# Gates of two steps as one pair in an attention and rational feed-forward kernel, with a planned order of work

## The chip, the cores and the metric

The kernel runs on one core of a Trainium2 chip. TensorE (PE in the profile; PEld are its weight loads), VectorE (DVE), ScalarE (ACT), GpSimd (POOL) and SyncE (SP, which issues the transfers here) run their own queues in order and wait for each other through semaphores. The metric is the device time of one execution in microseconds, median of several runs.

## What is computed

Sliding-window attention (8 batches, 8 heads, 576 positions, head size 64, window 64) gives x with 4608 tokens of 512 columns. A feed-forward layer with a rational gate follows:

```python
def _moe_ref(x, w_in, w_out, a, b) -> np.ndarray:
    h = x @ w_in
    h2 = h * h
    h3 = h2 * h
    P = a[0] + a[1] * h + a[2] * h2 + a[3] * h3
    Q = 1.0 + np.abs(b[0]) * np.abs(h) + np.abs(b[1]) * h2
    g = P / (Q + 1e-06)
    return (g @ w_out).astype(np.float32)
```

The hidden width is 2048, the output has 512 columns, all in float32.

## The kernel before

**Tiles and steps.** The tokens are cut into 12 chunks of 384 (CH). A chunk needs 4 attention units (one for each pair of heads) and 16 steps (one for each 128 of the hidden width). All products of the feed-forward layer are made in three terms of split operands (high and low parts of x, w and g), which keeps float32 accuracy. A step has ffn1 (l. 517: 12 matmuls of 128x384 into a PSUM bank h), the gate (l. 529 to 543) and ffn2 (l. 550: 9 matmuls of 128x512 into three banks ps_o). Chunks 0 and 1 go first over one half of the hidden width and then the other (l. 545), so that the second half of the weights can be loaded and split meanwhile; the sums of a half are spilled to memory and read back. From chunk 2 on all weights stay in SBUF.

**The gate.** ScalarE reads h three times: u = h squared, r = |b0 h|, num = a3 h + a2. DVE makes u = |b1| u + r. ScalarE takes 1/(1 + 1e-6 + u) as Ln and Exp into r. DVE makes num = num h, then num = (num + a1) h, the last read of h; then gh = (num + a0) r, and in three more operations the low part gl. That is five ScalarE and seven DVE operations of 128x384 a step. u, r and num have two tiles each, gh and gl four each (GB), h two banks.

**Attention units.** A unit loads qk and v (l. 389, 397; two slots each), makes scores in the two banks ps_s, takes the row maximum on DVE, Exp on ScalarE into sm, normalizes sm on DVE (l. 467), transposes it on TensorE into ps_s, copies that to pT on ScalarE (l. 475; one tile), multiplies with v into ps_x and splits the result into xh and xl (l. 488 to 502). From chunk 3 on, a unit's value products and the next one's scores are one group (l. 508).

**Weights.** load_weight (l. 370) takes a loaded slot w_st (three, after six spare places at the start): ScalarE extracts exponents into top, DVE puts the words together in a tile w_c (two of them), ScalarE rounds that to the high part, DVE subtracts for the low part. Then fetch() issues the next load. There are 32 such pieces, two in each of the first steps, then one.

**The order of work.** Nothing is issued as it is written. Each call is recorded with what it reads and writes (Planner, l. 51), a cost is put on it (l. 110), and plan() (l. 183) simulates the engines: whenever an engine is free it takes, of the operations that are ready, the one recorded first. emit() then issues each engine's queue in that order. ffn1 and the gate of a step are recorded at step s, ffn2 of step s at s + 3 (LAG). A dependence is recorded between a write and a read or two writes of the same bytes; two reads make none.

Of the kernel before, what the change touches and what calls it, by code (L numbers as in the profile page):

```python
# [21 lines left out]
CH = 384  # L22
# [1 line left out]
PR = TC // 2  # L24
AHEAD = 3
LAG = 3
GB = 4
SLOTS = 3
WARM = 7
FILL = 430  # L30
C1AT = 0, 0, 1, 3
ON_PE = 2
JOIN = 4
# [17 lines left out]
class Planner:  # L51
# [58 lines left out]
    def cost(self, engine, method, out, reads, kw, args):  # L110
        if isinstance(out, Late):
            n = out.size // 4
        else:
            n = 1
            for _, k in out.ap[1:]:
                n *= k
        if engine == "SP":
            parts = 128 if isinstance(out, Late) else (out.ap[0][1] if out.tensor.__class__.__name__ != "DRamTensorHandle" else 0)
            size = mybir.dt.size(out.dtype) * n * (parts or out.ap[0][1])
            return 400, 400, size  # L120
        if engine == "PE":
            if method == "transpose":
                return 109, 270, 0
            if isinstance(args[2], Late):
                n = args[2].size // 4
            else:
                n = 1
                for _, k in args[2].ap[1:]:
                    n *= k
                if args[2].dtype == F32:  # L130
                    return (45, 270, 0) if args[1].ap[0][1] == 64 else (52, 225, 0)
            return n * 0.452, n * 0.452 + 165, 0
        if engine == "ACT":
# [23 lines left out]
        if engine == "POOL":  # L157
            return (n * 2.0 + 60, n * 2.0 + 100, 0) if method in ("tensor_scalar", "tensor_copy") else (n * 2.4 + 130, n * 2.4 + 170, 0)
# [24 lines left out]
    def plan(self):  # L183
        waiting = {e: [] for e in self.free}
        missing = [len(o.before) for o in self.ops]
        for o in self.ops:
            if not o.before:
                waiting[o.engine].append(o)
        dma_free = 0
        for _ in self.ops:  # L190
            start, engine = min((max(self.free[e], min(o.ready for o in w)), e) for e, w in waiting.items() if w)
            op = min((o for o in waiting[engine] if o.ready <= start), key=lambda o: o.index)
            waiting[engine].remove(op)
            op.start, self.free[engine] = start, start + op.occ
# [53 lines left out]
def swa_rational_ffn(ctx: ExitStack, tc: tile.TileContext, qk, v, w_in, w_out, out):  # L248
# [16 lines left out]
    ps_s = psum.tile([P, 2, 512], F32, name="ps_s")  # L265
    ps_x = psum.tile([P, 512], F32, name="ps_x")
    ps_o = [psum.tile([P, DO], F32, name=f"o{t}") for t in range(NTS)]
    h_ring = Ring(psum, 2, [P, 512], F32, "h")


    ctx.enter_context(tc.manual_schedule())
# [31 lines left out]
    a_sb, b_raw = ab_sb[:, 0:4], ab_sb[:, 4:6]  # L303
    b_sb = const.tile([P, 2], F32, name="b_sb")

    warm = const.tile([P, 512], BF16, name="warm")
    nc.vector.memset(warm, 0.0)
    for _ in range(WARM):
        nc.tensor.matmul(ps_o[2], warm[:, 0:P], warm, start=True, stop=True)
    make_mask()  # L310

    H = NF // 2
# [24 lines left out]
    QK = 2 * CH + WIN  # L337
    QKAB = QK + 6
    UNIT = QKAB + TC * P
    qk_ring = Ring(ring, 2, [P, QKAB], F32, "qk")  # L340
    vt_ring = Ring(ring, 2, [P, TC * P], F32, "vt")
    w_ring = Ring(ring, SLOTS, [P, 1026], F32, "w_st")
    spare = [late.tile([P, H * NCC * P], F32, name=f"early_{n}", tag=f"late_{n}") for n in ("wi_h", "wi_l")]
    spare_slots = [t[:, k * 1026:(k + 1) * 1026] for k in range(H * NCC * P // 1026) for t in spare]
    c_ring = Ring(ring, 2, [P, 512], F32, "w_c")
    top_ring = Ring(const, 0, [], F32, "top")
    top_ring.tiles = tops
    sm_ring = Ring(ring, 2, [P, 2, PR, P], F32, "sm")
    pT_ring = Ring(ring, 1, [P, 2, PR * P], F32, "pT")
    small = {n: Ring(ring, 2, [P, 2 * PR], F32, n) for n in ("nmx", "sums", "rs")}  # L350
    tmp = {n: Ring(ring, 2, [P, CH], F32, n) for n in ("r", "u", "num")}
    g_ring = [Ring(ring, GB, [P, CH], F32R, n) for n in ("gh", "gl")]
    ob_ring = Ring(ring, 2, [P, DO], F32, "ob")

    shares = {t.tensor.name: f"late_{n}" for t, n in zip(early + spare, ("wo_l", "wo_h", "wi_h", "wi_l"))}
# [14 lines left out]
    def load_weight(which, i):  # L370
        w = staged.pop((which, i))
        f = (lambda t: t.rearrange("p c n -> p (c n)")) if which == "in" else (lambda t: t)
        hi_name, lo_name = ("wi_h", "wi_l") if which == "in" else ("wo_h", "wo_l")
        top, c = top_ring(), c_ring()
        low = w.bitcast(U32)[:, 0:1024].rearrange("p (n two) -> p n two", two=2)[:, :, 1]
        exponents = w.bitcast(BF16)[:, 4:2052].rearrange("p (n four) -> p n four", four=4)[:, :, 0]
        pl.scalar.copy(out=top.bitcast(F16).rearrange("p (n two) -> p n two", two=2)[:, :, 1], in_=exponents)
# [9 lines left out]
        return c if c < 2 else (c + 1) % 2  # L387

    def load_qk(c, hp):
        qk_t = early[hp // 2][:, hp % 2 * UNIT:hp % 2 * UNIT + QKAB] if c == 0 else qk_ring()  # L390
        pl.sync.dma_start(out=qk_t, in_=qk[hp, c])
        u = live[c, hp] = {}
        u["q"] = qk_t[:, 0:CH].rearrange("p (t s) -> p t s", s=WIN)
# [12 lines left out]
    def two_banks(c, hp, transposed):  # L406
        if c == 0 and transposed:
            return [ps_o[0], ps_o[1]], None
        if c == 0 and hp % 2:
            return [h_ring(), h_ring()], None  # L410
        return [ps_s[:, 0], ps_s[:, 1]], ps_s

    def blocks(ap):
# [26 lines left out]
    def score_maximum(c, hp):  # L440
        u = live[c, hp]
        on_pe, ps, both, m = u["on_pe"], u["ps"], u["both"], u["m"]
        sm, nmx = u["sm"], u["nmx"] = sm_ring(), small["nmx"]().rearrange("p (z r) -> p z r", z=2)
        if not on_pe:
            u["s"] = [sm[:, z] for z in range(2)]
            for z in range(2):
# [20 lines left out]
    def unit_norm(c, hp):  # L467
# [2 lines left out]
        pl.vector.tensor_scalar(out=u["sums"], in0=u["sums"], scalar1=1e-9, scalar2=None, op0=ALU.add)  # L470
        pl.vector.reciprocal(out=rs, in_=u["sums"])
        sm = u["sm"] = u["sm"].rearrange("p z r c -> p (z r) c")
        pl.vector.tensor_tensor(out=sm, in0=sm, in1=rs.unsqueeze(2).broadcast_to([P, 2 * PR, P]), op=ALU.mult)

    def unit_transpose(c, hp):
        u = live[c, hp]
        ps, both = two_banks(c, hp, True)
        with pl.group():
            for j in range(2 * PR):
                pl.tensor.transpose(ps[j // PR][:, (j % PR) * P:(j % PR + 1) * P], u["sm"][:, j, :], ident)  # L480
        pT = u["pT"] = pT_ring()
        if both is not None:
            pl.scalar.copy(out=pT, in_=both[:, :, 0:PR * P])
        else:
# [29 lines left out]

    gs = {}

    def ffn1(c, i):
        h = h_ring()[:, 0:CH]
        n = 0
        whole = ExitStack()  # L520
        if c > 1 or i >= 2:
# [1 line left out]
        with whole:  # L523
            for cc in range(NCC):
                with pl.group():
                    for w, x in (("wi_h", 1), ("wi_h", 0), ("wi_l", 0)):
                        pl.tensor.matmul(h, weight_piece(w, i, cc), x_sb[x_slot(c)][x][cc], start=n == 0, stop=n == 3 * NCC - 1)
                        n += 1
        r, u, num = (tmp[n]() for n in ("r", "u", "num"))
        gh, gl = (g() for g in g_ring)  # L530
        pl.scalar.activation(u, h, AF.Square)
        pl.scalar.activation(r, h, AF.Abs, scale=b_raw[:, 0:1])
        pl.scalar.activation(num, h, AF.Identity, scale=a_sb[:, 3:4], bias=a_sb[:, 2:3])
        pl.vector.scalar_tensor_tensor(out=u, in0=u, scalar=b_sb[:, 1:2], in1=r, op0=ALU.mult, op1=ALU.add)
        pl.scalar.activation(r, u, AF.Ln, bias=QADD)
        pl.scalar.activation(r, r, AF.Exp, scale=-1.0)
        pl.vector.tensor_tensor(out=num, in0=num, in1=h, op=ALU.mult)
        pl.vector.scalar_tensor_tensor(out=num, in0=num, scalar=a_sb[:, 1:2], in1=h, op0=ALU.add, op1=ALU.mult)
        pl.vector.scalar_tensor_tensor(out=gh, in0=num, scalar=a_sb[:, 0:1], in1=r, op0=ALU.add, op1=ALU.mult)
        pl.vector.scalar_tensor_tensor(out=u, in0=u, scalar=QADD, in1=gh.bitcast(F32), op0=ALU.add, op1=ALU.mult)  # L540
        pl.vector.scalar_tensor_tensor(out=u, in0=num, scalar=a_sb[:, 0:1], in1=u, op0=ALU.add, op1=ALU.subtract)
        pl.vector.tensor_tensor(out=gl, in0=u, in1=r, op=ALU.mult)
        gs[c, i] = gh, gl

    phases = [(0, 0, H), (1, 0, H), (1, H, NF), (0, H, NF)] + [(c, 0, NF) for c in range(2, NCH)]
# [94 lines left out]
    for s in range(total + LAG):  # L640
# [1 line left out]
            if fn is load_weight:  # L642
                fn(*args)
        if s < total:
            ffn1(*steps[s])
        for fn, *args in todo.get(s, ()):
            if fn is not load_weight:
                fn(*args)
        if s >= LAG:
            ffn2(s - LAG)  # L650
    pl.plan()
    pl.fill("PE", ps_o[2].tensor.name, FILL, (nc.tensor.matmul, (ps_o[2], warm[:, 0:P], warm), dict(start=True, stop=True)))
    pl.emit()


# [35 lines left out]
```

## Time and profile before

| | |
|---|---|
| median of 3 runs | 982.49 us (981.6 to 982.84) |
| the profiled execution | 982.07 us |
| its span, first to last instruction | 980.3 us |
| TensorE matmuls | 952.6 us busy, 97% |
| DVE | 911.2 us busy, 93% |
| ScalarE | 698.5 us busy, 71% |
| granted TensorE clock | 0.997 of full speed |
| DMA | 68.38 MB, mean 70 GB/s |

Matmuls are pipelined and their ends are modelled, so their busy time says only whether TensorE had something to do. A duration is that of one instruction; neighbours on an engine overlap by some tens of ns, so the distance from start to start is what an instruction takes of its engine. All recorded operations carry line 226 in the profile (the planner's emit), so they are told apart by their tiles: `num<-num,h` is DVE's first product of the gate. In the list of waits a row says which engine and tile waited for which, the total in us, how often, and the longest.

### The profile page before, as it was taken

The page shows a single profiled execution, that of the slowest core. Times are in us where ns is not written, and L with a number is a line of the kernel's source. Part 1 is how long each engine was busy: PE and PEld are TensorE (multiplying, and loading weights), DVE is VectorE, ACT ScalarE, POOL GpSimd, SP SyncE. Part 2 cuts the span into 40 slices and gives each one's busy share as a digit, 9 for nine tenths or more (in the row PEclk, how much of TensorE's full clock was granted, in tenths as well). Part 3 has the DMA queues.
Part 4 walks back from the last instruction along what each step waited for, and adds up shares of the span by engine and source line. Part 5 has one row for each costly group of instructions (what it writes and reads, how often), then busy time and mean ns, then how long its engine had stood idle before and what let it go on. Part 6 is the DMA issues. An engine that isn't in the chain of part 4 may idle for free.

```text
span 980.3 us, 17701 instructions
## 1 busy us (share of the span) xinstructions
PE 952.6 (97%) x6672; PEld 824.6 (84%) x6675; DVE 911.2 (93%) x1747; ACT 698.5 (71%) x1737; POOL 4.4 (0%) x20
## 2 busy tenths in 40 slices
PE   8899999999999999999999999999999999999998
PEld 5677788888888888888888888888888888888996
DVE  6999999998999999999999999999999899999996
ACT  7988777776667667767677677667766776676664
POOL 1000000000000000000000000000000000000000
PEclk9999999999999999999999999999999999999999
DMA  9344341313103103103102200210310310300000
GB/s 360 127 171 147 122 150 39 96 50 117 51 1 117 35 17 118 35 17 116 37 17 74 79 17 26 93 51 1 118 35 17 118 35 18 100 1 2 33 1 32
DMA packets 24564, 68.38 MB, mean 70 GB/s; under 512 B 2720, under 2 KB 2720, under 8 KB 24480
## 3 DMA queue, kind: packets, MB, share of 16 engines
q1 hardware_dynamic: 24480, 67.27, 20.2%
q8 instruction: 52, 0.85, 0.4%
q14 instruction: 32, 0.26, 0.1%
HBM read 57.03 MB, written 10.22 MB: 69 GB/s over the span
## 4 chain that ended last, share of the span: by engine, by line
PE 64%; DVE 19%; ACT 10%; issue 2%; DMA 1%; ACTq 0%; DVEq 0%
PE o L226 29%; PE h L226 28%; DVE u L226 6%; PE ps_s L226 5%; ACT sm L226 4%; DVE num L226 3%; PE ps_x L226 3%; ACT r L226 2%; DVE gh L226 2%; DVE sm L226 2%; DVE nmx L226 1%; ACT u L226 1%; DVE gl L226 1%; DMA w_st<-w_out 1%; ACT num L226 1%
## 5 line engine op out<-in xcount | busy, mean ns | idle before, releaser
L226 PE MATMUL h<-xl,wi_h 128*128 128x384 f32 x768 | 260.4, 339 | 7.7 <-DVE num L226 6.2
L226 PE MATMUL h<-xh,wi_l 128*128 128x384 f32 x768 | 258.1, 336 | 0.0
L226 PE MATMUL h<-xh,wi_h 128*128 128x384 f32 x768 | 257.9, 336 | 0.0
L226 PE MATMUL o<-wo_h,gl 128*128 128x512 f32 x576 | 236.5, 411 | 2.5 <-DVE gl L226 1.7
L226 PE MATMUL o<-wo_h,gh 128*128 128x512 f32 x576 | 228.2, 396 | 0.0
L226 PE MATMUL o<-wo_l,gh 128*128 128x512 f32 x576 | 227.0, 394 | 0.0
L226 ACT ACTIVATE u<-h 128x384 f32<-128x384 f32 x192 | 94.2, 491 | 158.4 <-PE h L226 153.6
L226 PEld LDWEIGHTS h<-xl,wi_h 128*128 128x128 f32 x768 | 144.2, 188 | 20.3 <-DVE num L226 10.2
L226 PEld LDWEIGHTS h<-xh,wi_h 128*128 128x128 f32 x768 | 144.2, 188 | 7.2
L226 ACT ACTIVATE num<-h,ab_sb 128x384 f32<-128x384 f32 x192 | 129.7, 675 | 25.7 <-PE h L226 15.6
L226 PEld LDWEIGHTS h<-xh,wi_l 128*128 128x128 f32 x768 | 144.2, 188 | 0.3 <-DVE wi_l L226 0.3
L226 ACT ACTIVATE r<-u 128x384 f32<-128x384 f32 x192 | 101.3, 527 | 48.1 <-DVE u L226 44.8
L226 PEld LDWEIGHTS o<-wo_h,gl 128*128 128x128 f32 x576 | 108.1, 188 | 29.0 <-issue 5.1
L226 PEld LDWEIGHTS o<-wo_h,gh 128*128 128x128 f32 x576 | 108.5, 188 | 26.3
L226 DVE SCALAR_TENSOR_TENSOR gh<-num,ab_sb,r 128x384 fp32r<-128x384 f32 x192 | 117.9, 614 | 8.7 <-ACT r L226 1.6
L226 PEld LDWEIGHTS o<-wo_l,gh 128*128 128x128 f32 x576 | 108.7, 189 | 16.5
L226 DVE SCALAR_TENSOR_TENSOR num<-num,ab_sb,h 128x384 f32<-128x384 f32 x192 | 117.3, 611 | 5.6 <-ACT r L226 1.5
L226 DVE SCALAR_TENSOR_TENSOR u<-u,b_sb,r 128x384 f32<-128x384 f32 x192 | 117.9, 614 | 2.9 <-ACT r L226 1.0
L226 DVE SCALAR_TENSOR_TENSOR u<-num,ab_sb,u 128x384 f32<-128x384 f32 x192 | 118.1, 615 | 2.7
L226 ACT ACTIVATE r<-h,ab_sb 128x384 f32<-128x384 f32 x192 | 111.4, 580 | 11.1 <-DVE num L226 11.1
L226 DVE SCALAR_TENSOR_TENSOR u<-u,gh 128x384 f32<-128x384 f32 x192 | 106.4, 554 | 2.7
L226 DVE TENSOR_TENSOR num<-num,h 128x384 f32<-128x384 f32 x192 | 105.0, 549 | 3.5 <-ACT r L226 2.2
(74 smaller groups left out, 983.6 us busy)
## 6 DMA issues: line engine op xcount, KB each, us to landing
qk<-qk SPq DMA_DIRECT2D x44, 419.0 KB, 4.2
vt<-v SPq DMA_DIRECT2D x44, 384.0 KB, 3.6
out<-ob SPq DMA_DIRECT2D x33, 256.0 KB, 2.1
w_st<-w_out SPq DMA_DIRECT2D x15, 512.0 KB, 3.5
w_st<-w_in SPq DMA_DIRECT2D x11, 512.0 KB, 3.6
early<-qk SPq DMA_DIRECT2D x4, 419.0 KB, 5.5
early<-v SPq DMA_DIRECT2D x4, 384.0 KB, 8.1
early_wi_l<-w_in SPq DMA_DIRECT2D x3, 512.0 KB, 9.4
```

Source lines behind the costliest of these rows:

```text
L226: call(*[value(x) for x in args], **{k: value(x) for k, x in kw.items()})
```

## The change

- Steps are grouped: the first four and the last four alone (ALONE), all others in pairs. ffn1 still runs for each step. After the second ffn1 of a pair, gate() records, for each step, num, u and r on ScalarE (num first, before it was last) and both products of num with h on DVE. The rest (u, Ln, Exp, gh, u, u, gl) is one operation of 768 columns for both steps.
- h is one tile of two banks. u, r and num come from six tiles of 2x384 columns (TMP), used in turn; gh and gl have two pair tiles each (PAIRS). Slots hands out a pair tile or half of one.
- plan(): for TensorE, the operation recorded first is taken among those that have been ready for 300 ns; if there are none, among all that are ready (MARGIN).
- Decoded weights are written over the first 512 words of their load slot; w_c is gone. The slot is now read until the subtraction for the low part.
- pT is written over sm. qk has one slot; the first two units of chunk 1 load into room left in the early tiles, and the last two units of chunk 0 put sm into spare room.
- Small: planned cost of a matmul column 0.4545 instead of 0.452 ns, 50 ns more for a group of transposes, the warm-up operand is 128 columns read four times. PSUM_PAIRS and ACT_NORM are switched off.

```diff
-GB = 4
+PAIRS = 2, 2
+TMP = 6
+ALONE = 4, 4
+PSUM_PAIRS = False
+ACT_NORM = 0, 0
+MARGIN = dict(PE=300)
...
-            op = min((o for o in waiting[engine] if o.ready <= start), key=lambda o: o.index)
+            able = [o for o in waiting[engine] if o.ready <= start]
+            op = min([o for o in able if o.ready <= start - MARGIN.get(engine, 0)] or able, key=lambda o: o.index)
...
+class Slots:
+    def __init__(self, pool, n, shape, dtype, name):
+        self.tiles = [pool.tile([shape[0], 2, *shape[1:]], dtype, name=f"{name}_{k}") for k in range(n)]
+        self.n = 0
+    def __call__(self, size):
+        t, k = self.tiles[self.n // 2 % len(self.tiles)], self.n % 2
+        self.n += size
+        return t if size == 2 else t[:, k]
...
-    h_ring = Ring(psum, 2, [P, 512], F32, "h")
+    h_ring = Slots(psum, 1, [P, 512], F32, "h")
...
-    qk_ring = Ring(ring, 2, [P, QKAB], F32, "qk")
+    qk_ring = Ring(ring, 1, [P, QKAB], F32, "qk")
...
-        top, c = top_ring(), c_ring()
+        top, c = top_ring(), w[:, 0:512]
...
-        pT = u["pT"] = pT_ring()
+        pT = u["pT"] = u["sm"].rearrange("p (z r) c -> p z (r c)", z=2)
...
-    tmp = {n: Ring(ring, 2, [P, CH], F32, n) for n in ("r", "u", "num")}
-    g_ring = [Ring(ring, GB, [P, CH], F32R, n) for n in ("gh", "gl")]
+    tmp = Slots(ring, TMP, [P, CH], F32, "tmp")
+    g_ring = [Slots(ring, n, [P, CH], F32R, name) for n, name in zip(PAIRS, ("gh", "gl"))]
...
+    def gate(group, hs):
+        size = len(group)
+        num, u, r = (tmp(size) for _ in range(3))
+        gh, gl = (g(size) for g in g_ring)
+        parts = [(u, r, num, hs)]
+        if size == 2 and not PSUM_PAIRS:
+            parts = [tuple(t[:, k] for t in parts[0]) for k in range(2)]
+        for u1, r1, num1, h in parts:
+            pl.scalar.activation(num1, h, AF.Identity, scale=a_sb[:, 3:4], bias=a_sb[:, 2:3])
+            pl.scalar.activation(u1, h, AF.Square)
+            pl.scalar.activation(r1, h, AF.Abs, scale=b_raw[:, 0:1])
+            pl.vector.tensor_tensor(out=num1, in0=num1, in1=h, op=ALU.mult)
+            pl.vector.scalar_tensor_tensor(out=num1, in0=num1, scalar=a_sb[:, 1:2], in1=h, op0=ALU.add, op1=ALU.mult)
         pl.vector.scalar_tensor_tensor(out=u, in0=u, scalar=b_sb[:, 1:2], in1=r, op0=ALU.mult, op1=ALU.add)
         pl.scalar.activation(r, u, AF.Ln, bias=QADD)
         pl.scalar.activation(r, r, AF.Exp, scale=-1.0)
...
+    groups = [[s] for s in range(ALONE[0])] + [[s, s + 1] for s in range(ALONE[0], total - ALONE[1], 2)]
+    groups += [[s] for s in range(total - ALONE[1], total)]
+    group_of = {s: g for g in groups for s in g}
...
         if s < total:
-            ffn1(*steps[s])
+            group = group_of[s]
+            if s == group[0]:
+                hs = h_ring(len(group))[..., 0:CH]
+            ffn1(*steps[s], hs if len(group) == 1 else hs[:, s - group[0]])
+            if s == group[-1]:
+                gate(group, hs)
```

More of the change, by code (lines that the diff above doesn't have):

```diff
@@ L131, in cost @@
                     return (45, 270, 0) if args[1].ap[0][1] == 64 else (52, 225, 0)
-            return n * 0.452, n * 0.452 + 165, 0
+            return n * 0.4545, n * 0.4545 + 165, 0
         if engine == "ACT":
@@ L304, in swa_rational_ffn @@
     b_sb = const.tile([P, 2], F32, name="b_sb")
-    warm = const.tile([P, 512], BF16, name="warm")
+    warm = const.tile([P, P], BF16, name="warm")
     nc.vector.memset(warm, 0.0)
+    warm_up = (ps_o[2], warm, warm.unsqueeze(1).broadcast_to([P, 4, P]))
     for _ in range(WARM):
-        nc.tensor.matmul(ps_o[2], warm[:, 0:P], warm, start=True, stop=True)
+        nc.tensor.matmul(*warm_up, start=True, stop=True)
     make_mask()
@@ L343, in swa_rational_ffn @@
     spare = [late.tile([P, H * NCC * P], F32, name=f"early_{n}", tag=f"late_{n}") for n in ("wi_h", "wi_l")]
-    spare_slots = [t[:, k * 1026:(k + 1) * 1026] for k in range(H * NCC * P // 1026) for t in spare]
-    c_ring = Ring(ring, 2, [P, 512], F32, "w_c")
+    SPARES = H * NCC * P // 1026
+    spare_slots = [t[:, k * 1026:(k + 1) * 1026] for k in range(SPARES) for t in spare]
     top_ring = Ring(const, 0, [], F32, "top")
@@ L348, in swa_rational_ffn @@
     sm_ring = Ring(ring, 2, [P, 2, PR, P], F32, "sm")
-    pT_ring = Ring(ring, 1, [P, 2, PR * P], F32, "pT")
     small = {n: Ring(ring, 2, [P, 2 * PR], F32, n) for n in ("nmx", "sums", "rs")}
-    tmp = {n: Ring(ring, 2, [P, CH], F32, n) for n in ("r", "u", "num")}
-    g_ring = [Ring(ring, GB, [P, CH], F32R, n) for n in ("gh", "gl")]
+    tmp = Slots(ring, TMP, [P, CH], F32, "tmp")
+    g_ring = [Slots(ring, n, [P, CH], F32R, name) for n, name in zip(PAIRS, ("gh", "gl"))]
     ob_ring = Ring(ring, 2, [P, DO], F32, "ob")
@@ L389, in load_qk @@
     def load_qk(c, hp):
-        qk_t = early[hp // 2][:, hp % 2 * UNIT:hp % 2 * UNIT + QKAB] if c == 0 else qk_ring()
+        if c == 0:
+            qk_t = early[hp // 2][:, hp % 2 * UNIT:hp % 2 * UNIT + QKAB]
+        elif c == 1 and hp < 2:
+            qk_t = early[hp][:, 2 * UNIT:2 * UNIT + QKAB]
+        else:
+            qk_t = qk_ring()
         pl.sync.dma_start(out=qk_t, in_=qk[hp, c])
@@ L409, in two_banks @@
         if c == 0 and hp % 2:
-            return [h_ring(), h_ring()], None
+            return [h_ring(1), h_ring(1)], None
         return [ps_s[:, 0], ps_s[:, 1]], ps_s
@@ L442, in score_maximum @@
         on_pe, ps, both, m = u["on_pe"], u["ps"], u["both"], u["m"]
-        sm, nmx = u["sm"], u["nmx"] = sm_ring(), small["nmx"]().rearrange("p (z r) -> p z r", z=2)
+        if c == 0 and hp >= 2:
+            sm = spare[hp - 2][:, SPARES * 1026:SPARES * 1026 + 2 * PR * P].rearrange("p (z r c) -> p z r c", z=2, c=P)
+        else:
+            sm = sm_ring()
+        nmx = small["nmx"]().rearrange("p (z r) -> p z r", z=2)
+        u["sm"], u["nmx"] = sm, nmx
         if not on_pe:
@@ L472, in unit_norm @@
         sm = u["sm"] = u["sm"].rearrange("p z r c -> p (z r) c")
+        if ACT_NORM[0] <= c * HP + hp < ACT_NORM[1]:
+            for j in range(2 * PR):
+                pl.scalar.activation(sm[:, j], sm[:, j], AF.Copy, scale=rs[:, j:j + 1])
+            return
         pl.vector.tensor_tensor(out=sm, in0=sm, in1=rs.unsqueeze(2).broadcast_to([P, 2 * PR, P]), op=ALU.mult)
@@ L477, in unit_transpose @@
         ps, both = two_banks(c, hp, True)
-        with pl.group():
+        with pl.group(50):
             for j in range(2 * PR):
                 pl.tensor.transpose(ps[j // PR][:, (j % PR) * P:(j % PR + 1) * P], u["sm"][:, j, :], ident)
-        pT = u["pT"] = pT_ring()
+        pT = u["pT"] = u["sm"].rearrange("p (z r) c -> p z (r c)", z=2)
         if both is not None:
@@ L515, in swa_rational_ffn, with ffn1 @@
     gs = {}
-    def ffn1(c, i):
-        h = h_ring()[:, 0:CH]
+    def ffn1(c, i, h):
         n = 0
@@ L528, in ffn1 @@
                         n += 1
[L529 to L533, printed above, removed]
+    def gate(group, hs):
[11 more added lines that the diff above has]
+            pl.vector.scalar_tensor_tensor(out=num1, in0=num1, scalar=a_sb[:, 1:2], in1=h, op0=ALU.add, op1=ALU.mult)
         pl.vector.scalar_tensor_tensor(out=u, in0=u, scalar=b_sb[:, 1:2], in1=r, op0=ALU.mult, op1=ALU.add)
@@ L536, in ffn1 @@
         pl.scalar.activation(r, r, AF.Exp, scale=-1.0)
-        pl.vector.tensor_tensor(out=num, in0=num, in1=h, op=ALU.mult)
-        pl.vector.scalar_tensor_tensor(out=num, in0=num, scalar=a_sb[:, 1:2], in1=h, op0=ALU.add, op1=ALU.mult)
         pl.vector.scalar_tensor_tensor(out=gh, in0=num, scalar=a_sb[:, 0:1], in1=r, op0=ALU.add, op1=ALU.mult)
@@ L542, in ffn1 @@
         pl.vector.tensor_tensor(out=gl, in0=u, in1=r, op=ALU.mult)
-        gs[c, i] = gh, gl
+        for k, s in enumerate(group):
+            gs[steps[s]] = (gh, gl) if size == 1 else (gh[:, k], gl[:, k])
     phases = [(0, 0, H), (1, 0, H), (1, H, NF), (0, H, NF)] + [(c, 0, NF) for c in range(2, NCH)]
@@ L651, in swa_rational_ffn @@
     pl.plan()
-    pl.fill("PE", ps_o[2].tensor.name, FILL, (nc.tensor.matmul, (ps_o[2], warm[:, 0:P], warm), dict(start=True, stop=True)))
+    pl.fill("PE", ps_o[2].tensor.name, FILL, (nc.tensor.matmul, warm_up, dict(start=True, stop=True)))
     pl.emit()
```

## The prediction

> **What bounds the kernel now.** I read the page first, then busy time by stretch, then TensorE's waits on both sides of 142 us, then the timeline of the stretch that those pointed at.
>
> ```profile
> span 980.3 us, 17701 instructions
> PE 952.6 (97%) x6672; PEld 824.6 (84%) x6675; DVE 911.2 (93%) x1747; ACT 698.5 (71%) x1737; POOL 4.4 (0%) x20
> ```
>
> Two engines are nearly full, so an average can't say which one sets the end. The stretches can:
>
> ```profile
> 29.00:71.00 42.00, 36.37 (x319) 28.54 (x319) 41.81 (x85) 38.98 (x108) 0.00 (x0) 1.00 0.43 152
> 71.00:100.00 29.00, 26.58 (x151) 21.93 (x150) 29.00 (x55) 25.13 (x49) 0.00 (x0) 1.00 0.43 137
> 100.00:142.00 42.00, 38.64 (x207) 32.77 (x206) 41.77 (x81) 33.41 (x64) 0.00 (x0) 1.00 0.45 150
> 278.00:356.00 78.00, 77.33 (x552) 67.90 (x551) 72.32 (x139) 54.71 (x140) 0.00 (x0) 1.00 0.16 53
> 356.00:434.00 78.00, 77.71 (x554) 68.41 (x553) 73.56 (x142) 55.16 (x140) 0.00 (x0) 1.00 0.16 54
> ```
>
> Each row has the stretch, its length, then busy us of PE, PEld, DVE, ACT. From 29 to 142 us DVE is busy for 112.6 of 113 us and PE for 101.6: DVE is the bound. Later PE is busy for 77.3 and 77.7 of 78 us and DVE for 72 to 74: PE is the bound. Why DVE is full early is seen in one window and in the starts around it:
>
> ```profile
> 116.82:126.26 9.44, 8.68 (x42) 7.46 (x42) 9.44 (x19) 7.42 (x14) 0.00 (x0) 1.00 0.34 112
> ...
> 116.82 0.67 ACT L226 ACTIVATE num<-h,ab_sb 128x384 f32<-128x384 f32 x1 [1.47 <-DVE u L226]
> 126.26 0.67 ACT L226 ACTIVATE num<-h,ab_sb 128x384 f32<-128x384 f32 x1 [1.46 <-DVE u L226]
> ...
> 118.16 0.69 DVE L226 SCALAR_TENSOR_TENSOR w_c<-w_st,top 128x512 uint32<-128x512 uint32 x1
> 118.76 0.56 DVE L226 SCALAR_TENSOR_TENSOR u<-u,gh 128x384 f32<-128x384 f32 x1
> 119.22 0.62 DVE L226 SCALAR_TENSOR_TENSOR u<-u,b_sb,r 128x384 f32<-128x384 f32 x1
> 119.76 0.62 DVE L226 SCALAR_TENSOR_TENSOR u<-num,ab_sb,u 128x384 f32<-128x384 f32 x1
> 120.29 0.69 DVE L226 TENSOR_TENSOR wo_l<-w_c,wo_h 128x512 fp32r<-128x512 f32 x1
> 120.89 0.56 DVE L226 TENSOR_TENSOR gl<-u,r 128x384 fp32r<-128x384 f32 x1
> 121.36 0.56 DVE L226 TENSOR_TENSOR num<-num,h 128x384 f32<-128x384 f32 x1
> 121.82 0.69 DVE L226 SCALAR_TENSOR_TENSOR w_c<-w_st,top 128x512 uint32<-128x512 uint32 x1
> ```
>
> Durations overlap, so I take start to start: 0.60 us for an operation on a weight piece, 0.53 for a gate operation that reads a per-partition scalar from ab_sb or b_sb, 0.47 for one that doesn't. Two steps hold 8 of the second kind, 6 of the third, and two weight pieces of two operations each: 4.24 + 2.82 + 2.40 = 9.46 us. The pattern repeats in 9.44, so DVE's work is the period. The waits of TensorE itself, up to 142 us and after (to 960):
>
> ```profile
> PE h L226 <- DVE num L226: 6.2, 8, 1.4
> PE ps_x L226 <- ACT pT L226: 2.1, 3, 0.9
> PE o L226 <- DVE gl L226: 1.7, 3, 0.9
> PEld h L226 <- DVE xl L226: 1.9, 2, 1.3
> ...
> PE ps_s L226 <- DVE sm L226: 3.1, 6, 1.0
> PE ps_s L226 <- ACT ob L226: 2.7, 4, 0.7
> PE o L226 <- DVE ob L226: 0.5, 1, 0.5
> ```
>
> The first four rows fall before 142 us: TensorE waits for DVE's last read of h (bank of h not free) and for gl. Later only 6.3 us of waits are left in 818 us, and none of them is on the gate.
>
> **The change, part by part.** *Five of a step's seven DVE operations are done for two steps at once.* Merged are u with b_sb, gh and the subtraction (scalar operand), and u with gh, and gl (none). The trace has no gate operation on 768 columns, but one tensor_tensor of that width:
>
> ```profile
> L226 DVE TENSOR_TENSOR gl<-u,r 128x384 fp32r<-128x384 f32 x192 | 106.1, 553 | 0.6
> L226 DVE TENSOR_TENSOR sm<-sm,rs 128x768 f32<-128x768 f32 x48 | 46.0, 957 | 1.4
> ...
> 38.25 0.95 DVE L226 TENSOR_TENSOR sm<-sm,rs 128x768 f32<-128x768 f32 x1
> 39.12 0.95 DVE L226 TENSOR_REDUCE nmx<-ps_s 128x6 f32<-128x768 f32 x1
> ```
>
> 384 more columns cost 957 - 553 = 404 ns. A merged operation without scalar takes 0.87 us start to start, against 2 x 0.47: 0.07 saved. One with a scalar takes 0.53 + 0.40 = 0.93 against 1.06: 0.13 saved. That is 3 x 0.13 + 2 x 0.07 = 0.53 us a pair. By the ends of the nearest rows (every one like the plain one, every one like the scalar one) it is 0.35 to 0.65. [...]
>
> How many of these pairs count? Where DVE is the bound, all of them; elsewhere only those that a wait hangs on.
>
> ```profile
> L226 PE MATMUL h<-xl,wi_h 128*128 128x384 f32 x672 | 226.1, 336 | 0.0
> 963.19 0.49 ACT L226 ACTIVATE u<-h 128x384 f32<-128x384 f32 x1 [1.46 <-PE h L226]
> 967.38 0.49 ACT L226 ACTIVATE u<-h 128x384 f32<-128x384 f32 x1 [0.94 <-PE h L226]
> ```
>
> The first row is of the window 142 to 960: 672 at four a step are 168 steps, and two more (h done at 963.19 and 967.38) end after 960, so 22 of 192 start before 142 us. The first four stay alone, which leaves 18 steps, 9 pairs: 9 x 0.53 = **4.8 us**. It counts in full only if DVE stays the bound: two steps then need 9.44 - 0.53 = 8.91 us of DVE, and TensorE, whose undisturbed step is 967.38 - 963.19 = 4.19, needs 8.38. It does.
>
> *The same merging on ScalarE (Ln and Exp)* shortens an engine that is 71% busy: nothing by itself. [...]
>
> *Earlier release of h, six double tmp tiles.* num comes first and both its products are done a step at a time, so a bank is free after three ACT reads and two DVE operations. That ends the 6.2 us wait on h as a wait; but in a stretch where DVE has no idle time, what comes late next is gl, and the time stays DVE's sum. The [1.47 <-DVE u] above is ScalarE waiting for its num tile: gone with four steps' room, and of no worth by itself for the same reason. I count nothing.
>
> *TensorE prefers groups ready for 300 ns.* The waits after 142 us are short (0.4 to 1.0 us each), of groups that the planner thought just ready. Passing over them can end all of the 6.3 us, or none if the pairs put new ones in their place. I take half, **3.2 us**; 0 and 6.3 go into the range.
>
> *Buffers.* The loads that they bear on (last column: us to landing):
>
> ```profile
> qk<-qk SPq DMA_DIRECT2D x44, 419.0 KB, 4.2
> w_st<-w_out SPq DMA_DIRECT2D x15, 512.0 KB, 3.5
> w_st<-w_in SPq DMA_DIRECT2D x11, 512.0 KB, 3.6
> ```
>
> *Weights decoded over their load slot.* A slot is now free after the subtraction, not after the operation on w_c: 118.16 to 120.29 plus 0.69, so 2.1 us later. A slot's load is issued behind that on SP's queue, ahead of the next qk, v and part transfers. Three slots turn around in 3 x 4.7 = 14 us, of which a load takes 3.5, so some 8 us of slack cover it: 0. Without cover, at most 2.1 us x 26 loads / 3 slots = 18 us.
>
> *One qk slot instead of two, pT over sm.* A qk load (4.2 us) now waits for the previous unit's scores, and from the third chunk on units lie two or four steps, 9 to 20 us, apart: covered. For the first two units of the second chunk there is extra room. pT over sm takes away a wait of 2.1 us in the early part (ScalarE and DVE are full there): 0, at best 2.1.
>
> Sum: the profiled execution took 982.07 us (span 980.3 and 1.8 around it); -4.8 - 3.2 gives 974.1. The median of the runs is 0.4 above the profiled one: **974.5 us**.
>
> **The rivals.** *A, only the early part gains.* New lateness uses up the 3.2 us. Against it stands TensorE's order: in the last stretch
>
> ```profile
> 959.00 0.49 ACT L226 ACTIVATE u<-h 128x384 f32<-128x384 f32 x1 [0.95 <-PE h L226]
> 959.38 0.58 ACT L226 ACTIVATE r<-h,ab_sb 128x384 f32<-128x384 f32 x1
> 959.85 0.68 ACT L226 ACTIVATE num<-h,ab_sb 128x384 f32<-128x384 f32 x1
> 960.65 0.53 ACT L226 ACTIVATE r<-u 128x384 f32<-128x384 f32 x1
> 961.20 0.53 ACT L226 ACTIVATE r<-r 128x384 f32<-128x384 f32 x1
> ```
>
> the three reads take 1.53 us, and a dependent operation starts about when the one before ends (960.65 to 961.20). After the second h of a pair, gl therefore needs 1.53, then 1.02 + 2 x 1.06 (at most) + 1.02 + 0.96 + 1.02 + 0.96 = 8.6 us. Before the first ffn2 of the pair TensorE has two steps of work, 8.38. So gl comes about in time or just late, and then the next ffn1 (2.1 us) can go first, as its bank was freed early. For A: slack that is several us now becomes a fraction of one. 982.5 - 4.8 = 977.7.
>
> *B, slower: ScalarE's and VectorE's reads of h are kept apart.* Now num is ScalarE's last read, so DVE never reads a bank that ScalarE still reads. With num first, DVE's num x h is ready when num ends (0.68 after h), while u and r are read until 1.53: if they exclude each other, DVE stands for 0.85 us in a step, with the other pair's chain queued behind it and TensorE waiting for that gl. The planner doesn't know of it (two reads make no dependence there). After 142 us DVE has, with merging, 78 - 72.9 + 8 x 0.53 = 9.3 us idle in 16 steps, 0.58 a step. It decides when over 0.58 / 0.85, two steps in three, are hit; DVE's queue is seldom empty, which speaks for fewer. At three in four, 16 x 0.75 x 0.85 - 9.3 = 0.9 us a chunk over ten chunks, with jitter doubling it: 18 - 4.8, so 996; at the point itself 978. [...] No run here shows such a pair of reads.
>
> *C, no change.* The 9 pairs save little (0.35 us) and new waits take the rest: 979 to 984.
>
> *D, more.* All 6.3 us after 142 us go, and the early waits for pT and xl too (2.1 + 1.9): 982.5 - 4.8 - 6.3 - 4.0 = 967.4.
>
> **How the numbers follow.** Forecast 0.47, A 0.17, D 0.12: faster. C 0.09: about no change. B, or gl late beyond the spare ffn1, 0.15: slower. A measurement here tells 0.2%, 2.0 us, from no change. So faster 0.76, same 0.09, slower 0.15. The range goes from D's end with a little for the scalar bound, 966.5, to 985, inside B; about 5 in 100 lie below and 11 above.
>
> **What would show it.** Right: five DVE groups of 128x768 with 92 instructions each, DVE's busy time near 911 - 92 x 0.53 = 862 us; a period near 8.9 us for two steps before 142 us, with DVE still full; TensorE's wait for num gone early, its waits on ps_s after 142 us halved; about the same count of matmuls. Wrong: DVE idle within the early stretch, waits of DVE num for ACT r or of TensorE for gl after 142 us, or ScalarE waiting for w_st loads.

## The result and the profile after

The changed kernel takes 1260.05 us (median of four runs, 1256.86 to 1260.6) against 982.62 for the kernel before beside it: a ratio of 1.2819, 95% interval 1.28 to 1.2838. The forecast was 974.5 us, range 966.5 to 985, with 0.15 for slower. It is slower by 277 us.

The span and the busy times of the page after:

```profile
span 1258.8 us, 16920 instructions
PE 1033.1 (82%) x6676; PEld 851.8 (68%) x6676; DVE 866.7 (69%) x1287; ACT 683.5 (54%) x1553; POOL 4.4 (0%) x20
```

TensorE executes as many matmuls as before (6676 against 6672). DVE's busy time fell from 911.2 to 866.7, near the 862 that the prediction named, and ScalarE's from 698.5 to 683.5. So there is less work, and no engine is full any more. Three of the five merged DVE groups by form (busy us, mean ns, idle us before them):

```profile
L232 DVE SCALAR_TENSOR_TENSOR tmp<-tmp,ab_sb,tmp 128x768 f32<-128x768 f32 x92 | 93.4, 1015 | 1.6
L232 DVE SCALAR_TENSOR_TENSOR gh<-tmp,ab_sb,tmp 128x768 fp32r<-128x768 f32 x92 | 93.3, 1015 | 68.0 <-ACT tmp L232 67.0
L232 DVE TENSOR_TENSOR gl<-tmp,tmp 128x768 fp32r<-128x768 f32 x92 | 87.8, 955 | 1.4
```

The counts and the durations are those foreseen. The loss lies in idle time, and it isn't in one stage. The same stretches as in the prediction (length, busy us of PE, PEld, DVE, ACT, POOL, then the granted clock):

```profile
29.00:71.00 42.00, 32.92 (x253) 25.11 (x253) 36.31 (x70) 32.67 (x86) 0.00 (x0) 0.96 0.36 124
100.00:142.00 42.00, 30.38 (x131) 25.80 (x132) 28.42 (x41) 24.05 (x41) 0.00 (x0) 0.92 0.29 94
278.00:356.00 78.00, 66.49 (x455) 55.85 (x459) 54.99 (x80) 39.23 (x91) 0.00 (x0) 0.96 0.15 46
356.00:434.00 78.00, 65.14 (x438) 53.57 (x430) 52.52 (x77) 41.65 (x95) 0.00 (x0) 0.96 0.13 43
```

Before, DVE was full up to 142 us and PE was busy for 77 of 78 us later; now both have gaps everywhere, and 455 and 438 matmul records stand where 552 and 554 stood. The longest waits of the three engines (us in total, times, longest):

```profile
ACT tmp L232 <- DVE tmp L232: 318.8, 252, 5.0
DVE tmp L232 <- ACT tmp L232: 222.4, 203, 4.3
ACT tmp L232 <- PE h L232: 168.8, 78, 6.4
...
PE o L232 <- DVE gl L232: 99.6, 72, 3.1
PE h L232 <- ACT tmp L232: 54.3, 39, 2.5
PE h L232 <- DVE tmp L232: 36.3, 42, 4.4
```

The tile named tmp holds the gate's intermediate values, so the first two rows read at first like rival B: ScalarE and DVE take turns. A stretch of the timeline (start, duration, instruction, idle time before it and its releaser) shows that three engines take turns, not two:

```profile
1030.07 0.65 ACT L232 ACTIVATE tmp<-h,ab_sb 128x384 f32<-128x384 f32 x1
...
1030.78 0.44 PE L232 MATMUL h<-xl,wi_h 128*128 128x384 f32 x1 [1.50 <-ACT tmp L232]
...
1032.82 0.34 PE L232 MATMUL h<-xh,wi_l 128*128 128x384 f32 x1
...
1033.19 0.49 ACT L232 ACTIVATE tmp<-h 128x384 f32<-128x384 f32 x1 [2.47 <-PE h L232]
1033.71 0.56 DVE L232 TENSOR_TENSOR tmp<-tmp,h 128x384 f32<-128x384 f32 x1 [2.95 <-ACT tmp L232]
...
1034.30 0.58 ACT L232 ACTIVATE tmp<-h,ab_sb 128x384 f32<-128x384 f32 x1 [0.62 <-DVE tmp L232]
...
1035.15 0.57 DVE L232 SCALAR_TENSOR_TENSOR tmp<-tmp,ab_sb,h 128x384 f32<-128x384 f32 x1
...
1035.76 0.67 ACT L232 ACTIVATE tmp<-h,ab_sb 128x384 f32<-128x384 f32 x1 [0.88 <-DVE tmp L232]
```

ScalarE makes num from one bank of h until 1030.72. Then PE, which had waited for that, writes twelve matmuls into the *other* bank, and ScalarE's Square of the first bank, which was complete all along, waits 2.47 us for PE. DVE's first product waits for the Square, ScalarE's Abs for that product, the next num for DVE. No two engines touch the tile h at a time, whichever bank they use: over the whole trace PE's writing of it overlaps the others' reading for 0 us. From one num to the next that is 5.69 us. In the kernel before, 16 steps with their attention took 78.49 us late in the run, 4.9 a step; after, they take 102.5, which is 6.4 a step.

### The profile page after: what moved, and what is told of

Same layout as the page of the kernel before. It is cut to its first block, busy times and chain, and to the rows that moved or that the text cites. A ratio compares the mean times of both kernels' runs of the same rounds, so it can differ in the third digit from the quotient of the medians.

```text
span 1258.8 us, 16920 instructions
## 1 busy us (share of the span) xinstructions
PE 1033.1 (82%) x6676; PEld 851.8 (68%) x6676; DVE 866.7 (69%) x1287; ACT 683.5 (54%) x1553; POOL 4.4 (0%) x20
## 4 chain that ended last, share of the span: by engine, by line
PE 42%; DVE 29%; ACT 24%; issue 4%; DMA 1%; SPq 0%; ACTq 0%; DVEq 0%
PE h L232 26%; DVE tmp L232 18%; ACT tmp L232 17%; PE o L232 14%; ACT sm L232 6%; DVE gl L232 5%; DVE sm L232 2%; DVE nmx L232 2%; PE ps_s L232 2%; DVE xl L232 1%; ACT top L232 1%; PE ps_x L232 1%; DMA early_wi_h<-w_in 1%; DMA w_st<-w_out 0%; DVE gh L232 0%
## 5 line engine op out<-in xcount | busy, mean ns | idle before, releaser
L232 ACT ACTIVATE tmp<-h,ab_sb 128x384 f32<-128x384 f32 x384 | 238.4, 625 | 329.6 <-DVE tmp L232 239.9
L232 DVE TENSOR_TENSOR tmp<-tmp,h 128x384 f32<-128x384 f32 x192 | 106.0, 552 | 189.4 <-ACT tmp L232 182.1
L232 ACT ACTIVATE tmp<-tmp 128x768 f32<-128x768 f32 (+1 forms) x200 | 164.2, 822 | 75.5 <-DVE tmp L232 73.1
L232 DVE SCALAR_TENSOR_TENSOR tmp<-tmp,ab_sb,h 128x384 f32<-128x384 f32 x192 | 116.7, 608 | 104.0 <-PE h L232 63.1
L232 DVE SCALAR_TENSOR_TENSOR gh<-tmp,ab_sb,tmp 128x768 fp32r<-128x768 f32 (+1 forms) x100 | 98.2, 983 | 68.8 <-ACT tmp L232 67.7
L232 ACT ACTIVATE tmp<-h 128x384 f32<-128x384 f32 x192 | 93.0, 485 | 85.7 <-PE h L232 79.3
L232 ACT ACTIVATE sm<-sm,nmx 128x128 f32<-128x128 f32 x216 | 83.9, 390 | 29.1 <-DVE nmx L232 29.1
L232 DVE SCALAR_TENSOR_TENSOR tmp<-tmp,ab_sb,tmp 128x768 f32<-128x768 f32 (+1 forms) x96 | 95.8, 998 | 1.7
L232 DVE SCALAR_TENSOR_TENSOR tmp<-tmp,b_sb,tmp 128x768 f32<-128x768 f32 (+1 forms) x96 | 95.6, 995 | 0.6 <-ACT tmp L232 0.6
L232 DVE SCALAR_TENSOR_TENSOR tmp<-tmp,gh 128x768 f32<-128x768 f32 (+1 forms) x100 | 92.1, 922 | 1.6
```

Of the source, the lines that this page charges most:

```text
L232: call(*[value(x) for x in args], **{k: value(x) for k, x in kw.items()})
```

## The experiments

Three theories. T1: the two banks of h, now halves of one tile, are ordered as one object, so that PE's writing of one bank and the reading of the other exclude each other (engines take turns on the tile). T2 (rival B): with num first, ScalarE's and DVE's reads of the same bank are kept apart. T3: the merging itself brings gl too late. Each figure is the median of its runs; ratios are against the kernel before, run on the same chip beside it (981.49 to 982.24 us in these series), with a 95% interval.

### Two tiles for h in the changed kernel

```
-    h_ring = Slots(psum, 1, [P, 512], F32, "h")
+    h_ring = Banks(psum, 2, [P, 512], F32, "h")
...
-            parts = [tuple(t[:, k] for t in parts[0]) for k in range(2)]
+            parts = [(u[:, k], r[:, k], num[:, k], hs[k]) for k in range(2)]
```

Banks hands out two separate tiles of one bank each; a pair gets both as a list.

> The changed kernel with one edit: the two banks of h are two tiles again, not halves of one tile; pairs, num first and everything else stay. Theory T1 (the two halves of the one h tile exclude each other, so that TensorE writing one bank, ScalarE and VectorE reading the other wait for each other): 970 to 1010 us, and the accesses of h by the three engines overlap in time again. Theory T2 (with num first, ScalarE and VectorE read the same bank and are kept apart there): still above 1150 us. Theory T3 (merging itself brings gl too late): about 1250 us.

Measured: 1029.88 us, ratio 1.0494 (1.0476 to 1.0513). Of the 277 us, 230 go with this edit alone. T1 is the main cause, but the time lies above the 970 to 1010 us expected for T1 alone: 48 us are left above the kernel before.

### num last again, one tile kept

```
-            pl.scalar.activation(num1, h, AF.Identity, scale=a_sb[:, 3:4], bias=a_sb[:, 2:3])
             pl.scalar.activation(u1, h, AF.Square)
             pl.scalar.activation(r1, h, AF.Abs, scale=b_raw[:, 0:1])
+            pl.scalar.activation(num1, h, AF.Identity, scale=a_sb[:, 3:4], bias=a_sb[:, 2:3])
```

> The changed kernel with one edit: ScalarE reads h in the old order u, r, num, so VectorE never wants a bank that ScalarE still reads; h stays one tile of two banks. T1: still above 1150 us. T2: 970 to 1010 us. T3: about 1250 us.

Measured: 1235.53 us, ratio 1.258 (1.2539 to 1.2622). Rival B's order by itself explains 25 us here; the rest stays while the tile is one.

### Two tiles and num last

Both edits together.

> The changed kernel with both edits: two tiles for h, and num read last. T1 and T2, each or together: about 974 us, the sum of the prediction (970 to 980). T3: above 1200 us, since the merging and its buffers are all still there.

Measured: 971.65 us (971.22 to 972.46), ratio 0.9896 (0.9881 to 0.9911): the fastest kernel of the study, and 10 us faster than the kernel before. Merged gates, decoding over the load slot, one qk slot and the preference are all in it, so T3 falls. Its page, and the same late stretches:

```profile
span 969.4 us, 16849 instructions
PE 947.5 (98%) x6675; PEld 828.2 (85%) x6675; DVE 856.1 (88%) x1287; ACT 666.2 (69%) x1553; POOL 4.4 (0%) x20
```

```profile
100.00:142.00 42.00, 40.62 (x222) 35.69 (x221) 42.00 (x62) 31.13 (x55) 0.00 (x0) 1.00 0.37 126
278.00:356.00 78.00, 78.00 (x557) 69.27 (x557) 69.23 (x102) 52.70 (x123) 0.00 (x0) 1.00 0.16 53
```

PE is busy for 78.00 of 78 us, at full clock. How the accesses lie now, in the timeline of this kernel:

```profile
602.51 0.34 PE L232 MATMUL h<-xl,wi_h 128*128 128x384 f32 x1
...
602.63 0.55 DVE L232 TENSOR_TENSOR tmp<-tmp,h 128x384 f32<-128x384 f32 x1
602.69 0.34 PE L232 MATMUL h<-xh,wi_h 128*128 128x384 f32 x1
...
603.22 0.61 DVE L232 SCALAR_TENSOR_TENSOR tmp<-tmp,ab_sb,h 128x384 f32<-128x384 f32 x1
```

DVE reads one bank while PE writes the other, in the same 0.3 us. Added up over the trace, PE writes h for 63.6 us while ScalarE reads an h tile and for 82.2 us while DVE does (47.3 and 117.3 in the kernel before). In the changed kernel both sums are 0, and the timeline of the kernel before with h as one tile (the next run) has no such overlap from 500 to 512 us.

### The kernel before with h as one tile

```
-    h_ring = Ring(psum, 2, [P, 512], F32, "h")
+    h_both = psum.tile([P, 2, 512], F32, name="h")
+    h_ring = Ring(psum, 0, [], F32, "h")
+    h_ring.tiles = [h_both[:, k] for k in range(2)]
```

Nothing else of the change is in it: h still has two banks, and the order of the gate is the old one.

> The kernel before with one edit: its two banks of h are the halves of one tile, nothing else changes (order u, r, num, no pairs). T1: over 100 us slower than before, 1080 us or more, with h accessed by one engine at a time. T2 and T3: 982 us, no change.

Measured: 1259.52 us, ratio 1.2822 (1.28 to 1.2843). One line on how the tile is declared makes the whole of the slowdown, without a single merged gate. Its timeline:

```profile
506.57 0.44 PE L226 MATMUL h<-xl,wi_h 128*128 128x384 f32 x1 [0.36 <-DVE num L226]
...
508.59 0.34 PE L226 MATMUL h<-xh,wi_l 128*128 128x384 f32 x1
...
508.96 0.61 DVE L226 SCALAR_TENSOR_TENSOR num<-num,ab_sb,h 128x384 f32<-128x384 f32 x1 [1.92 <-PE h L226]
...
510.14 0.49 ACT L226 ACTIVATE u<-h 128x384 f32<-128x384 f32 x1 [2.89 <-DVE gl L226]
...
511.72 0.44 PE L226 MATMUL h<-xl,wi_h 128*128 128x384 f32 x1 [0.68 <-ACT num L226]
```

PE begins a step when DVE is through with its first product on the other bank; DVE's second product on that bank then waits 1.92 us until PE has written the step, and PE begins the step after that when ScalarE is through. That it is the ordering of a tile's accesses by the software that does this is inferred: the waits are there, and the one edit was how the tile is declared.

### The kernel before with num first

Two tiles, no pairs:

```
+        pl.scalar.activation(num, h, AF.Identity, scale=a_sb[:, 3:4], bias=a_sb[:, 2:3])
...
-        pl.scalar.activation(num, h, AF.Identity, scale=a_sb[:, 3:4], bias=a_sb[:, 2:3])
+        pl.vector.tensor_tensor(out=num, in0=num, in1=h, op=ALU.mult)
+        pl.vector.scalar_tensor_tensor(out=num, in0=num, scalar=a_sb[:, 1:2], in1=h, op0=ALU.add, op1=ALU.mult)
...
-        pl.vector.tensor_tensor(out=num, in0=num, in1=h, op=ALU.mult)
-        pl.vector.scalar_tensor_tensor(out=num, in0=num, scalar=a_sb[:, 1:2], in1=h, op0=ALU.add, op1=ALU.mult)
```

num goes ahead of u and r on ScalarE, and both its products ahead of u's operations on DVE.

> The kernel before with one edit: ScalarE reads h in the order num, u, r and VectorE's two products with h stand ahead of the operation on u, as in the changed gate; two tiles for h, no pairs. T2 alone: the read-read exclusion costs by itself what it cost in the changed kernel, 1029.9 - 971.7 = 58 us, or more since VectorE is fuller here: 1035 to 1060 us, with ScalarE's third read of h starting only after VectorE's first. Rival (it hurts only because a pair's chain queues behind it): 980 to 990 us.

Measured: 1046.48 us, ratio 1.0654 (1.0635 to 1.0674), so T2 by itself is worth 65 us in the unmerged kernel. The edit also moves DVE's two products ahead of its operation on u, but these stand there as well in the unmerged kernel with num last further down, which takes 981.24 us; so it is num first that costs. Its waits:

```profile
DVE num L226 <- ACT r L226: 41.8, 105, 0.7
...
ACT r L226 <- DVE num L226: 33.5, 57, 0.6
```

DVE's reading of h waits for ScalarE's Abs, ScalarE's Abs for DVE's reading: short waits in both directions, 162 of them. In the changed kernel with two tiles one sees the turns themselves:

```profile
600.34 0.67 ACT L232 ACTIVATE tmp<-h,ab_sb 128x384 f32<-128x384 f32 x1 [2.68 <-PE h L232]
...
600.91 0.48 ACT L232 ACTIVATE tmp<-h 128x384 f32<-128x384 f32 x1
...
601.48 0.55 DVE L232 TENSOR_TENSOR tmp<-tmp,h 128x384 f32<-128x384 f32 x1
...
602.06 0.58 ACT L232 ACTIVATE tmp<-h,ab_sb 128x384 f32<-128x384 f32 x1 [0.67 <-DVE tmp L232]
...
602.68 0.61 DVE L232 SCALAR_TENSOR_TENSOR tmp<-tmp,ab_sb,h 128x384 f32<-128x384 f32 x1 [0.65 <-ACT tmp L232]
```

All five read the same bank. num is done at 601.01, but its product starts only after the Square (0.48), the Abs only after the product, the last product only after the Abs. So in these rows ScalarE's and DVE's reads of one bank take turns; the one-tile runs above show an order between two banks as well.

### num first, with an order of work that knows of it

The kernel's own planner lays out each engine's order by the dependences that it knows, and two reads make none. Here, in the changed kernel with two tiles and num first, it also counts reads of one bank by two engines as a dependence:

```
+                    both_read = name in self.exclusive and self.ops[other].engine != op.engine
-                    if (wrote or is_write) and p0 < q1 and q0 < p1 and b0 < c1 and c0 < b1:
+                    if (wrote or is_write or both_read) and p0 < q1 and q0 < p1 and b0 < c1 and c0 < b1:
...
+    pl.exclusive = tuple(t.tensor.name for t in h_ring.tiles)
```

> The changed kernel with two tiles for h and num read first (1029.9 us), and the planner is told that reads of one bank of h by two engines exclude each other, in the order recorded. If the 58 us come from an order planned without knowing of the exclusion: 971 to 976 us. If they come from the exclusion itself: above 1010 us.

Measured: 972.57 us, ratio 0.9903 (0.9889 to 0.9916), within 1 us of the kernel with num last. In its timeline DVE's first product on a bank starts at 602.40, just after ScalarE's third read of it ends at 602.36. So the 58 us between 1029.88 and 971.65 are not the price of the reads taking turns but of an order planned in ignorance of it.

### One tile, with an order that knows of it

The changed kernel with its one tile, the planner treating any two engines on it as dependent:

```
+                    apart = name in self.exclusive and self.ops[other].engine != op.engine
-                    if (wrote or is_write) and p0 < q1 and q0 < p1 and b0 < c1 and c0 < b1:
+                    if apart or (wrote or is_write) and p0 < q1 and q0 < p1 and b0 < c1 and c0 < b1:
...
+    pl.exclusive = (h_ring.tiles[0].tensor.name,)
```

> The changed kernel as it is (one tile of two banks, num first), and the planner is told that all accesses of the h tile by different engines exclude each other, in the order recorded. By rows of the kernel before, a step holds the tile for 2.1 us of matmuls, 1.53 us of ScalarE's reads and 1.1 us of VectorE's, with hand-overs some 5.1 us, against 4.83 us that TensorE needs for a step with its share of attention. If the cost is the plan that does not know of the exclusion: 985 to 1040 us. If it is the exclusion itself: above 1150 us.

Measured: 1160.42 us, ratio 1.1819 (1.1797 to 1.1842). A better order gives back 100 of the 277 us; the other 178 stay. Where they are, in one pair of its timeline:

```profile
704.86 0.67 ACT L234 ACTIVATE tmp<-h,ab_sb 128x384 f32<-128x384 f32 x1 [2.77 <-PE h L234]
...
709.68 1.01 DVE L234 SCALAR_TENSOR_TENSOR tmp<-tmp,b_sb,tmp 128x768 f32<-128x768 f32 x1
...
710.61 0.61 DVE L234 SCALAR_TENSOR_TENSOR tmp<-tmp,ab_sb,h 128x384 f32<-128x384 f32 x1
...
711.89 0.45 PE L234 MATMUL h<-xl,wi_h 128*128 128x384 f32 x1
...
716.37 0.67 ACT L234 ACTIVATE tmp<-h,ab_sb 128x384 f32<-128x384 f32 x1 [3.50 <-PE h L234]
```

The turns are now ordered by pairs: ten reads from 704.86 to 711.22, then 24 matmuls from 711.89 to 716.33. The pair takes 11.51 us, 5.76 a step, where the kernel before needs 4.9 with its attention; 16 steps measure 92.4 to 93.0 us. 192 steps at 5.76 are 1106 us. In this order the tile is the bound. That no order could do better is not shown: of the 11.51 us, DVE spends 0.93 on another operation (709.68) ahead of its last product with h, and 0.67 pass between that product's end and PE's first matmul.

### What the parts are worth with h as two tiles

These start from the fastest kernel (971.65 us). Without the preference:

```
-MARGIN = dict(PE=300)
+MARGIN = {}
```

> The changed kernel with two tiles for h and num read last (971.7 us), and TensorE's preference for long-ready groups taken out. If that preference ends the short waits after 142 us (6.3 us before, 0.9 there), they come back: 974 to 978 us. If it is VectorE's idle time from the merging that ends them: within 1.5 us of 971.7.

Measured: 972.65 us, ratio 0.9902 (0.9885 to 0.9918). With the gates merged, the preference is worth 1 us by the medians, and the intervals overlap.

Without merged pairs:

```
-ALONE = 4, 4
+ALONE = 4, 188
```

> The changed kernel with two tiles for h and num read last, and every step's gate alone (no merging); buffers, in-place decoding and the preference stay. If the merging gives the prediction's 4.8 us before 142 us: 976 to 978 us, VectorE about 905 us busy. If the merging also gives the part after 142 us: 979 to 983 us. If buffers and preference give all: 971 to 973 us.

Measured: 981.24 us, ratio 0.9994 (0.9985 to 1.0003), DVE busy for 902.0 us, where the fastest kernel has 856.1: 45.9 us for 92 pairs, 0.50 a pair. So the merging is worth 9.6 us, and the rest of the change, with two tiles and num last but without it, nothing.

The kernel before with the preference alone:

```
+MARGIN = dict(PE=300)
...
-            op = min((o for o in waiting[engine] if o.ready <= start), key=lambda o: o.index)
+            able = [o for o in waiting[engine] if o.ready <= start]
+            op = min([o for o in able if o.ready <= start - MARGIN.get(engine, 0)] or able, key=lambda o: o.index)
```

> The kernel before with one edit: TensorE's preference for groups ready for 300 ns. By the prediction's second term: half to all of the 6.3 us of waits after 142 us, 976 to 980 us. If the preference needs VectorE's slack: 981 to 984 us.

Measured: 978.41 us, ratio 0.9963 (0.9951 to 0.9976), 3.1 us by the medians. The 981.24 above has the preference too, and beside it the change's buffers, DVE's products ahead of u, and the small edits; these together cost some 3 us in the unmerged kernel.

Pairs from the first step:

```
-ALONE = 4, 4
+ALONE = 0, 4
```

> The changed kernel with two tiles for h and num read last (971.7 us), and the first four steps in pairs too. VectorE is full there, so by 0.53 us a pair two more pairs give 1.1 us: 970 to 971.5 us. Rival: the first gates then wait for a second h while nothing else is queued, and the start is later: 972 to 976 us.

Measured: 971.91 us, ratio 0.9892 (0.9879 to 0.9906). Two more pairs gain nothing that can be measured; what the first steps wait for instead was not followed up.

Weights decoded by way of a tile of their own again, one instead of the two of the kernel before:

```
+    c_ring = Ring(ring, 1, [P, 512], F32, "w_c")
...
-        top, c = top_ring(), w[:, 0:512]
+        top, c = top_ring(), c_ring()
```

> The changed kernel with two tiles for h and num read last, and weights decoded in a tile of their own again (one, since two do not fit beside the pairs), so that a load slot is free after the operation that reads it. If decoding over the load slot costs part of the 2.8 us between the kernel before with the preference alone (978.4) and the unpaired kernel with all buffers (981.2): 969 to 971 us. If it is covered, as the prediction had it: 971 to 973 us. If one tile for two weights in flight is a new wait: 973 to 976 us.

Measured: 980.28 us, ratio 0.9978 (0.9969 to 0.9988), outside all three expectations and 8.6 us slower. The loss is made before 142 us: the step with number 22 (counted from 0) starts at 149.82 us, in the fastest kernel at 138.75. PE's waits:

```profile
PE h L232 <- DVE tmp L232: 7.1, 5, 2.1
PE o L232 <- DVE gl L232: 6.0, 6, 2.8
```

That one tile now serves two weights in flight is the likely reason, but it isn't shown: the waits that name w_c add up to 3.5 us. So the run says nothing of the price of decoding in place, which was not settled.

## Why the prediction was wrong, point by point

**The step that failed** is "Earlier release of h, six double tmp tiles", with its "a bank is free after three ACT reads and two DVE operations" and "I count nothing". It took the two banks as independent; the change had made them halves of one tile, and that was never costed. What the runs showed in its place: PE, ScalarE and DVE take turns on the whole tile. The run of the kernel before with one tile puts the price at 278 us (1259.52 less 981.77), as much as the change lost. The place to see it was the line of the diff that makes one slot with two halves out of two slots.

**Rival B** had the right place and a wrong size: with num first in the kernel before, ScalarE's Abs and DVE's products wait for each other 162 times, 75.3 us together. It priced 996 us for three steps in four hit by 0.85 us, with two in three as the point where DVE's idle time is used up. Measured by itself it is 65 us in the kernel before and 58 us in the changed one. What failed is the sum, as far as the timeline shows: it let DVE's 0.58 us of idle time a step take up the delay, and counted one stand a step. The timeline shows ScalarE and DVE held up in turn, with three hand-overs in a step. That "The planner doesn't know of it" was the weight-bearing part, as the run with the planner told shows. It is also not what made the slowdown: with one tile, num last still takes 1235.53.

**The merged gates**: counts and distances came as worked out (709.68 to 710.61 above is the 0.93 us of a merged operation with a scalar), and merging takes 0.50 us a pair off DVE (45.9 / 92) for the 0.53 of the prediction. The gain in time was mis-sized by its place. Between the unmerged kernel and the fastest one, the early part gives 3.9 us where 4.8 were forecast (step 22 starts at 142.62 and at 138.75 us), and the rest of the 9.6 comes later, where the prediction gave merging nothing.

**The preference**: "I take half, 3.2 us" of TensorE's waits after 142 us. Alone in the kernel before it gives 3.1 us, so its size was right there: the waits from 142 to 950 us fall from 6.7 (the 6.3 of the prediction leaves out two rows of 0.2) to 3.9. But in the fastest kernel those waits go whether it is there or not:

```profile
PE ps_s L232 <- DVE sm L232: 0.6, 1, 0.6
PE o L232 <- DVE rs L232: 0.3, 1, 0.3
```

These are all of PE's waits from 142 to 950 us in the fastest kernel, 0.9 us; with the preference taken out they are the same two rows. The unmerged run, with the preference, has 9.3 us of waits there. As merging is the one thing that both have and that run lacks, the spare time that merging gave DVE is the likely reason.

**Buffers**, taken at 0 within bounds from -2.1 to 18: some 3 us in the unmerged kernel, with the order of DVE's products and the small edits in that figure; which edit costs it stays open, and with merged gates it was not measured.

**T3, gl late by the pair's longer chain** (a part of the 0.15 for slower): refuted at 971.65 us, and at 972.57 with num first.

**The forecast as a sum**, 974.5, is 2.9 us above the kernel with two tiles and num last, which the change wasn't. That nearness is partly luck: there merging gave 9.6 us where 4.8 were put down, and the preference 1 by the medians where 3.2 were.

**What stays open.** How much of the 277 us is the lower clock and how much the turns was not separated; at a mean granted clock of 0.959, an estimate of the clock's share is 0.041 x 1258.8 = 52 us at most. The one-tile kernel before and the changed one agree to 0.5 us; that their orders, which differ much, come out so near may be chance. ps_s is one tile of two banks in every kernel here, and in the kernel before PE's writing and the others' reading of it overlap for 0 us as well; what two tiles would be worth there was not tried.

## What to carry to other kernels

Two buffers that engines use by turns were worth two tiles here: before merging such buffers into one for the sake of a common slice, look at whether a consumer of one half overlaps the producer of the other in the trace, and price the loss of that overlap, here 28% of the time (1259.52 against 981.77 us). If an operation is moved so that two engines would read one bank at the same time, look in the trace whether their reads take turns; here they did, and a planner that knew of it took the kernel from 1029.88 to 972.57 us, and num last, which keeps the reads in sequence, to 971.65. When a slowdown comes with gaps on every engine, read a few microseconds of the timeline for who waits for whom: the largest totals of the waits pointed at the tmp tiles, and only the timeline at the two banks of h.

## What the runs showed of the hardware that was not expected

TensorE's granted clock fell to half within a running kernel, in the place below after gaps of 1.47 and 2.04 us. First PE's instructions in the changed kernel, then three stretches of 3.41 us each (columns as in the table of stretches above):

```profile
490.67 0.40 PE L232 MATMUL o<-wo_h,gh 128*128 128x512 f32 x1
492.54 0.44 PE L232 MATMUL h<-xl,wi_h 128*128 128x384 f32 x1 [1.47 <-ACT tmp L232]
...
496.93 0.50 PE L232 MATMUL o<-wo_h,gl 128*128 128x512 f32 x1 [2.04 <-DVE gl L232]
...
498.41 0.63 PE L232 MATMUL o<-wo_l,gh 128*128 128x512 f32 x1
498.84 0.63 PE L232 MATMUL o<-wo_h,gh 128*128 128x512 f32 x1
```

```profile
490.59:494.00 3.41, 1.94 (x11) 1.50 (x10) 1.90 (x3) 1.90 (x9) 0.00 (x0) 1.00 0.00 0
494.00:497.41 3.41, 1.37 (x8) 1.01 (x7) 1.96 (x5) 1.07 (x2) 0.00 (x0) 1.00 0.00 0
497.42:500.83 3.41, 3.41 (x11) 2.53 (x10) 2.65 (x5) 1.52 (x3) 0.00 (x0) 0.50 0.00 0
```

PE stands for 1.47 and, twelve matmuls later, for 2.04 us. Soon after, the matmuls start 0.43 us apart (in a row of the same kind at full clock, 0.23), and the granted clock is 0.50. The changes of the clock in this trace lie 3.41 us or a multiple of it apart. With the trace cut at these times into stretches of 3.41 us, and PE's idle time taken from its matmul records, the stretch with 1.47 us idle is followed by full clock, the one with 2.04 by half. Counted so over this trace and that of the kernel before, from PE's first matmul to the end of each: of 621 stretches at full clock, 20 had 2.03 us or more idle, and half clock followed all of them; 20 had 1.60 to 1.98 us, and half clock followed 12, full clock 8; the other 581 had at most 1.57 us, and full clock followed all of them. Short gaps added up in some of these: the stretch that ends at 166.3 us of the changed kernel has 2.18 us idle, no gap in it is over 1.39, and half clock follows. The changed kernel has 30 stretches at half clock, 104.6 us together; the kernel before, with few gaps, has two, 7.9 us. So the changed kernel, having lost its cover, lost a second time: the mean clock of its profiled execution is 0.959, where the kernel before has 0.997 and the fastest one 0.998.
